# Opening of a spectral filter plus gated MLP kernel: first row tile in two halves on two queues, identity on GpSimd's queue, one dependency less, half a copy on VectorE

## The chip, the cores and the metric

The kernel runs on one core of one Trainium2 chip. The core has TensorE (PE; its weight loads are shown as PEld), VectorE (DVE), ScalarE (ACT), GpSimd (POOL) and SyncE (SP), and 16 DMA engines that SP, ACT and GpSimd can hand transfers to. The metric is the device time of one execution in microseconds (us); several runs are made and their median is given. One execution was also profiled, and that trace is what the prediction reads.

## What is computed

One input x of 2048 tokens by 512 channels (bf16) goes through two branches, whose results are added to it. Branch A layer-normalises x, takes a two-dimensional real FFT, multiplies by a complex filter and transforms back. Branch B is a gated MLP on the same normalised x.

```python
def reference(A_x, A_w_r, A_w_i, B_x, B_w_gate, B_w_up, B_w_down):
    ...
    x = A_x
    xn = _layernorm(x, axis=-1)
    # A: irfft2(rfft2(xn) * (w_r + 1j * w_i))
    # B: (gelu(xn @ w_gate) * (xn @ w_up)) @ w_down
    return x + _A_ref(xn, A_w_r, A_w_i) + _B_ref(xn, B_w_gate, B_w_up, B_w_down)
```

B_x is not used. The gate and up weights are 512 by 1792, the down weight 1792 by 512.

## The kernel before

**Tiling.** x is held as 16 row tiles of 128 partitions by 512 channels: token a*128+q is partition q of tile a. This text calls tile 0 "row one", tile 1 "row two" and so on. For every tile the kernel computes mean and variance on VectorE (`stats`: L520 and L521), the reciprocal root of the variance (`root_act` with ScalarE's square root and VectorE's reciprocal, L525 and L527, for rows one and two; `root_pool` on GpSimd for the others), the normalised tile (`norm`, L537), and its transpose (four 128 by 128 blocks), since TensorE needs channels on partitions. Rows two to four are transposed on TensorE with an identity matrix (`turn`, L550) and copied out of PSUM by VectorE (L555). Rows from five on are transposed by DMA. Row one has its own function, `first_half`, called for h=0 and h=1: 256 channels are normalised (L570), two blocks transposed on TensorE (L567) and copied by ScalarE (L572), so that the first half can go on before the second.

**The matmuls.** The gated MLP is 14 chunks of 128 hidden features by four blocks of four row tiles. `first(3)` starts chunks 0 to 2 on rows one and two as soon as each arrives (L734); everything after that in branch B is `gated` (L715, matmuls with wg and wu, evicted by ScalarE at L720 and L721, multiplied by VectorE at L722) and `down` (L763). Branch A's transforms are matmuls with constant matrices and butterflies on VectorE; TensorE fills the time between them with the MLP. Before its first real work TensorE runs eleven warm-up matmuls on a constant (L476), ten of 512 columns and one of 256.

**The order.** No order is written out. Every operation is declared with an engine, a planned cost, a key, what it reads and writes, and sometimes an explicit predecessor (`after`), a due time, or a planned landing (`land`) for a transfer. `_Sched.run` then lays out all engines in planned time: over all ready operations it takes the one that can start earliest, and among those of the same engine that could start within 0.05 us of it the one with the smallest key (ready time plus the given key, or the due time). This fixes each engine's instruction order. `_Sched.emit` then makes the waits: one semaphore per engine and one per transfer. An operation waits on the semaphores of its predecessors, on its own engine's too, where an older operation's result is read or where `after` names it. An engine runs its queue in order, so an instruction that waits holds all behind it. A changed planned time can change the order anywhere later.

**The transfers of the opening.** On ACT's queue: the identity with one further constant block (`small[:, 0:2]`, 64 KB), then the first 384 columns of wg and of wu. On SP's queue: row one, row two (128 KB each), then, gated behind the fourth warm-up matmul, rows three and four, columns 384 to 768 of wg and wu, rows five to eight, and so on in larger pieces. On GpSimd's queue: no transfer; its first operations are the memsets of `eps` (read by the square root), of `half` (read by `root_pool`) and of the filter's padding (L690).

**The dependency that the change touches.** In the lines

```python
        stats(0, -60.0)
        stats(1, -66.0, None, (sch.ops[-1],))
        root_act(0, 1, -75.0, (sch.ops[-2],))
        root_act(1, 1, -64.0)
```

`sch.ops[-1]` is row one's aggregate (L521), and `sch.ops[-2]` is row two's statistics (L520), so the reciprocal of row one (L527) is declared to come after row two's statistics.

Of the kernel before, what the change touches and what calls it, by code (L numbers as in the profile page):

```python
# [7 lines left out]
ACT = mybir.ActivationFunctionType  # L8
# [7 lines left out]
P = 128  # L16
# [128 lines left out]
class _Sched:  # L145
# [11 lines left out]
    def op(self, eng, cost, fn, reads=(), writes=(), tiles=(), key=0.0, after=(), dma=0, lag=0.0, due=None, land=None):  # L157
        o = _Op()
        o.eng, o.fn, o.cost, o.key, o.dma, o.lag, o.due, o.land = eng, fn, cost, key, dma, lag, due, land
        o.reads, o.writes, o.tiles = reads, writes, [(t, False) for t in tiles]  # L160
        o.extra = [a for a in after if a is not None]
        o.seq = len(self.ops)
        o.end = None
        o.pos = None
        self.ops.append(o)
        return o
# [184 lines left out]
def bass_parallel_sum__spectral_gfnet__glu_gated_geglu__prompt_kernel(  # L351
# [11 lines left out]
    c_small = nc.inline_tensor(small_np, name="c_small")  # L363
# [3 lines left out]
    xb = A_x[0].rearrange("(a q) d -> q a d", q=P)  # L367
# [5 lines left out]
    sch = _Sched()  # L373
    op = sch.op

    with ExitStack() as es:
        def sb(name, shape, dt=BF16, cell=0):
            n = int(np.prod(shape))
            t = es.enter_context(nc.sbuf_tensor(name, [P, n], dt))
            return view(t, name, 0, shape, cell)  # L380
# [13 lines left out]
        x = sb("x_sb", [16, D])  # L394
# [4 lines left out]
        small = sb("smallc", [9, P])  # L399
# [11 lines left out]
        rs = sb("rstd", [16], F32)  # L411
# [49 lines left out]
        def dma(q, dst, src, nbytes, wr=None, rd=None, key=0.0, after=(), cost=0.41, lag=0.0, land=None):  # L461
            after = tuple(after) + tuple(gate if q == "sp" else ())
            return op(q, cost, lambda e: e.dma_start(dst() if callable(dst) else dst.ap, src() if callable(src) else src.ap),
                      reads=rd if rd is not None else (), writes=wr if wr is not None else (), dma=nbytes, key=key, after=after, lag=lag, land=land)
# [16 lines left out]
        def load(q, dst, src, nbytes, **kw):  # L481
            return dma(q, dst, lambda: src, nbytes, wr=(dst,), **kw)

        def wload(q, dst, src, lo, hi, **kw):
            return load(q, dst[:, :, lo:hi], src[:, :, lo:hi], (hi - lo) * 1024, **kw)

        k = iter(np.arange(0.0, 1.0, 0.001))
        def rows(lo, hi, land=None):
            return load("sp", x[:, lo:hi], xb[:, lo:hi, :], (hi - lo) * 131072, key=next(k), land=land)

        load("act", small[:, 0:2].rs([2 * P]), c_small.ap()[:, 0:2 * P], 65536, key=-9)
        for w, v in ((wg, wgv), (wu, wuv)):
            wload("act", w, v, 0, 384, key=0.5, land=5.5 if w is wg else 6.4)
        rows(0, 1)
        rows(1, 2)
        gate.append(warms[3])
        for i in (2, 3):
            rows(i, i + 1, 6.3 + 0.3 * i)
# [14 lines left out]
        def xs(s):  # L513
            return x[:, s]

        def xn(s):
            return RB(8192 + 512 * (s % 8), [4, P])

        def stats(s, key, due=None, after=()):
            op("dve", 0.61, lambda e: e.bn_stats(bst[:, s].ap, xs(s).ap), reads=(xs(s),), writes=(bst[:, s],), key=key, due=due, after=after)  # L520
            op("dve", 0.11, lambda e: e.bn_aggr(bag[:, s].ap, bst[:, s].ap), reads=(bst[:, s],), writes=(bag[:, s],), key=key, due=due)  # L521

        def root_act(s0, n, key, after=()):
            sl = slice(s0, s0 + n)
            op("act", 0.29, lambda e: e.activation(rs.ap[:, sl], bag.ap[:, sl, 1], ACT.Sqrt, bias=eps.ap, scale=1.0),  # L525
               reads=(bag[:, sl], eps), writes=(rs[:, sl],), key=key)
            op("dve", 0.09, lambda e: e.reciprocal(rs.ap[:, sl], rs.ap[:, sl]), reads=(rs[:, sl],), writes=(rs[:, sl],), key=key, after=after)  # L527

        def root_pool(s0, n, key):
            sl = slice(s0, s0 + n)  # L530
# [26 lines left out]
        def first_half(h):  # L557
            cs = slice(2 * h, 2 * h + 2)
            i, r, o = xs(0)[:, 256 * h:256 * h + 256], xn(0)[:, cs].rs([256]), xnT[:, 0, 0, cs].rs([256])
            t = _T("sp")  # L560

            def bank():
                return ps_sp_bf[:, t.slot * 2048:t.slot * 2048 + 256]

            def f(e):
                for j in range(2):
                    ins = e.transpose(bank()[:, j * P:(j + 1) * P], xn(0).ap[:, 2 * h + j], ident.ap)  # L567
                return ins

            op("dve", 0.2, lambda e: e.tensor_scalar(r.ap, i.ap, bag.ap[:, 0, 0:1], rs.ap[:, 0:1], SUB, MUL), reads=(i, bag[:, 0], rs[:, 0:1]), writes=(r,), key=-70.0)  # L570
            op("pe", 2 * 0.107, f, reads=(r, ident), tiles=(t,), key=-70.0, lag=0.1)
            op("act", 0.27, lambda e: e.activation(o.ap, bank(), ACT.Copy), writes=(o,), tiles=(t,), key=-70.0)  # L572

        def turn_dma(s):
            i, o = xn(s), xnT[:, s // 4, s % 4]
# [63 lines left out]

        stats(0, -60.0)  # L640
        stats(1, -66.0, None, (sch.ops[-1],))
        root_act(0, 1, -75.0, (sch.ops[-2],))
        root_act(1, 1, -64.0)
        for h in range(2):
            first_half(h)
# [195 lines left out]
        for v, hh in ((4, (12, 13)), (0, (14, 15)), (2, (8, 9)), (6, (10, 11)), (1, (0, 1)), (7, (4, 6)), (3, (2, 7)), (5, (5, 3))):  # L841
            t = _T("sp")
# [17 lines left out]
        for ri, f in ((0, ADD), (1, SUB)):  # L860
            op("pool", 0.3, lambda e, ri=ri, f=f: e.tensor_tensor(edge.ap[:, ri], ev[0].ap[:, ri], ev[1].ap[:, ri], f),
               reads=(ev[0][:, ri], ev[1][:, ri]), writes=(edge[:, ri],), key=1.0)
# [53 lines left out]
        for i, v in enumerate((0, 4, 1, 7, 2, 6, 3, 5)):  # L916
            t = _T("sp")

            def f_i(e, v=v, t=t):
# [15 lines left out]
               writes=(gv,), tiles=(t,), key=-0.5)  # L935
# [40 lines left out]
        for jq in range(4):  # L976
# [4 lines left out]
            for jp in (2 * jq, 2 * jq + 1):  # L981
                t = _T("sp")
# [57 lines left out]
```

## Time and profile before

| what | value |
|---|---|
| median of 3 runs | 171.54 us (171.25 to 171.77) |
| the profiled execution | 171.33 us, of which 169.5 us is the span from first to last instruction |
| granted TensorE clock, mean | 1.00 |
| DMA, whole kernel | 15.62 MB, mean 92 GB/s |

The opening, by the timeline (start in us from the span's start; the engine's instructions in their order):

| engine | instructions |
|---|---|
| SP, issues | row one 0.72, row two 1.17, row three 2.65, row four 3.02, wg 3.50, wu 3.98 |
| ACT | issues identity 0.72, wg 1.12, wu 1.67; table load 2.29 (1.28 long); root of row one 4.29, of row two 5.29; copies L572 at 6.05 and 6.33 (0.38 each) |
| GpSimd | memsets of eps 0.72, half 0.75, filter 0.79 |
| VectorE | L520 3.35, L521 4.07, L520 4.29, L527 5.02, L521 5.10, L570 5.22 and 5.48 (0.34 each), L527 5.74, L537 5.92, L555 7.03 |
| TensorE | warm-up from 0.76, the last one starts 4.98; L567 5.62 (four), L734 6.49 (two), L550 6.61 (four), L734 from 6.83 |

A row of the profile's group views reads: line, engine, operation, what is written and read (by the kernel's names), shapes, count, then busy time and the mean of one. In a chain of waits each row is start, length and the work that the end of the kernel was waiting for then. "In queue q10" in a DMA view is ACT's queue, q1 is SP's.

### The profile page before, as it was taken

What the parts mean: (1) busy time and instruction counts of PE and PEld (TensorE: products, weight loads), DVE (VectorE), ACT (ScalarE), POOL (GpSimd) and SP (SyncE); (2) the same over time, 40 slices, a digit from 0 to 9 for tenths busy, and PEclk for the clock granted to TensorE, in tenths of its full rate; (3) what the DMA queues carried; (4) which work ended last, traced back from release to release, by engine and by line L of the source; (5) the groups of instructions that cost most, each with busy time, mean ns of one, the idle gap of its engine ahead of it and who ended that gap; (6) DMA issues with size and microseconds to landing.
All of it is one profiled execution on the core that took longest, in us unless ns stands there. A gap on an engine that the chain in (4) does not pass through costs nothing.

```text
span 169.5 us, 2696 instructions
## 1 busy us (share of the span) xinstructions
PE 166.0 (98%) x999; PEld 86.1 (51%) x999; DVE 146.0 (86%) x292; ACT 106.6 (63%) x175; POOL 11.3 (7%) x25
## 2 busy tenths in 40 slices
PE   8899999999999999999999999999999999999994
PEld 3598544445556443444444554644445654444443
DVE  2789999995975999999999999999999969963932
ACT  3688766663979739489663695875738896561000
POOL 2042243500000000010000000000000000000000
PEclk9999999999999999999999999999999999999999
DMA  5999999994025362420000000000000003300322
GB/s 152 333 346 352 283 129 311 216 261 95 0 51 114 84 134 74 116 119 2 0 0 0 0 4 0 0 0 0 4 0 2 0 4 104 128 15 0 124 67 63
DMA packets 22239, 15.62 MB, mean 92 GB/s; under 512 B 9165, under 2 KB 21714, under 8 KB 22226
## 3 DMA queue, kind: packets, MB, share of 16 engines
q1 hardware_dynamic: 21026, 14.60, 34.8%
q10 hardware_dynamic: 1200, 0.85, 1.7%
q8 instruction: 8, 0.13, 0.4%
q14 instruction: 5, 0.04, 0.1%
HBM read 11.38 MB, written 2.10 MB: 80 GB/s over the span
## 4 chain that ended last, share of the span: by engine, by line
PE 95%; DMA 2%; DVE 1%; ACT 0%; issue 0%
PE ps_gu L715 56%; PE ps_dn L763 21%; PE ps_sp L763 7%; PE ps_sp L988 2%; PE ps_sp L632 2%; PE ps_sp L847 2%; DMA x_sb<-in_A_x_dram 2%; PE ps_gu L734 1%; PE ps_sp L928 1%; PE ps_sp L929 1%; DVE bst L520 1%; PE ps_dn L734 1%; PE ps_sp L550 0%; PE ps_sp L851 0%; PE ps_sp L567 0%; ACT xnT L572 0%
## 5 line engine op out<-in xcount | busy, mean ns | idle before, releaser
L715 PE MATMUL ps_gu<-xnT,wg 128*128 128x512 bf16 (+1 forms) x236 | 56.7, 363 | 0.0
L715 PE MATMUL ps_gu<-xnT,wu 128*128 128x512 bf16 (+1 forms) x236 | 56.7, 363 | 0.0
L720 ACT ACTIVATE gg<-ps_gu 128x512 bf16<-128x512 f32 (+1 forms) x59 | 33.7, 572 | 12.2 <-PE ps_gu L715 10.5
L721 ACT ACTIVATE uu<-ps_gu 128x512 bf16<-128x512 f32 (+1 forms) x59 | 33.9, 575 | 10.5 <-PE ps_gu L715 10.2
L763 PE MATMUL ps_dn<-wd,hT 128*128 128x512 bf16 x168 | 38.9, 379 | 0.0
L467 DVE TENSOR_TENSOR specB<-specB 128x512 bf16<-128x512 bf16 (+2 forms) x58 | 33.6, 610 | 1.7 <-ACT specB L993 1.4
L715 PEld LDWEIGHTS ps_gu<-xnT,wu 128*128 128x128 bf16 x236 | 22.9, 98 | 23.0
L715 PEld LDWEIGHTS ps_gu<-xnT,wg 128*128 128x128 bf16 x236 | 22.6, 98 | 22.0 <-ACT uu L721 0.4
L763 PEld LDWEIGHTS ps_dn<-wd,hT 128*128 128x128 bf16 x168 | 16.3, 98 | 19.1
L722 DVE TENSOR_TENSOR hT<-gg,uu 128x512 bf16<-128x512 bf16 (+1 forms) x59 | 23.0, 394 | 1.9 <-ACT uu L721 1.8
L771 ACT ACTIVATE db<-ps_dn 128x512 bf16<-128x512 f32 x12 | 7.2, 597 | 18.4 <-PE ps_dn L763 18.4
L520 DVE BATCH_NORM_STATS2 bst<-x_sb 128x6 f32<-128x512 bf16 x16 | 11.0, 686 | 3.4 <-DMA x_sb<-in_A_x_dram 3.3
L467 DVE TENSOR_TENSOR specC<-specB 128x1024 bf16<-128x1024 bf16 (+2 forms) x18 | 12.4, 713 | 0.2
L763 PE MATMUL ps_sp<-wd,hT 128*128 128x512 bf16 (+2 forms) x70 | 12.3, 336 | 0.0
L467 DVE TENSOR_TENSOR specB<-specA 128x2048 bf16<-128x2048 bf16 x8 | 9.4, 1217 | 2.7 <-ACT specA L637 2.7
L772 DVE TENSOR_TENSOR x_sb<-db,x_sb 128x512 bf16<-128x512 bf16 x12 | 5.0, 418 | 5.3 <-ACT db L771 5.3
L763 PEld LDWEIGHTS ps_sp<-wd,hT 128*128 128x128 bf16 x70 | 6.4, 98 | 6.1 <-DVE x_sb L774 0.2
L467 DVE TENSOR_TENSOR specB<-specB,filt 128x2048 bf16<-128x2048 bf16 x8 | 9.4, 1220 | 0.0
L856 ACT ACTIVATE specA<-ps_sp 128x1024 bf16<-128x1024 f32 x8 | 7.8, 1035 | 1.3 <-PE ps_sp L847 1.3
L637 ACT ACTIVATE specA<-ps_sp 128x1024 bf16<-128x1024 f32 x8 | 7.7, 1023 | 1.2 <-PE ps_sp L632 1.2
L993 ACT ACTIVATE specB<-ps_sp 128x1024 bf16<-128x1024 f32 x8 | 7.8, 1031 | 0.8 <-PE ps_sp L988 0.8
L934 ACT ACTIVATE specC<-ps_sp 128x1024 bf16<-128x1024 f32 x8 | 7.8, 1039 | 0.0
(70 smaller groups left out, 128.8 us busy)
## 6 DMA issues: line engine op xcount, KB each, us to landing
out_dram<-x_sb SPq DMA_DIRECT2D x15, 128.0 KB, 1.8
wd<-in_B_w_down_dram SPq DMA_DIRECT2D x1, 1792.0 KB, 8.4
x_sb<-in_A_x_dram SPq DMA_DIRECT2D x3, 512.0 KB, 8.5
wg<-in_B_w_gate_dram SPq DMA_DIRECT2D x2, 512.0 KB, 8.6
wu<-in_B_w_up_dram SPq DMA_DIRECT2D x2, 512.0 KB, 9.2
toki<-c_ti SPq DMA_DIRECT2D x1, 768.0 KB, 4.4
tokf<-c_tf SPq DMA_DIRECT2D x1, 576.0 KB, 4.8
x_sb<-in_A_x_dram SPq DMA_DIRECT2D x4, 128.0 KB, 3.5
```

What stands on the lines that cost most here:

```text
L467: return op("dve", c_tt(n), lambda e: e.tensor_tensor(o.ap, a.ap, b.ap, f), reads=(a, b), writes=(o,), key=key, **kw)
L520: op("dve", 0.61, lambda e: e.bn_stats(bst[:, s].ap, xs(s).ap), reads=(xs(s),), writes=(bst[:, s],), key=key, due=due, after=after)
L637: op("act", c_act(1024), lambda e, yv=yv, t=t: e.activation(yv.ap, spair(t).rearrange("p (s r i) -> p s i r", s=4, r=4), ACT.Copy), writes ...
L715: ins = e.matmul(gub(t, n), w.ap[:, dc, fc * P:(fc + 1) * P], xnT.ap[:, b, sl, dc, :], start=(dc == 0), stop=(dc == 3))
L720: op("act", c_act(n), lambda e: e.activation(gg.ap[:, gs.slot, 0:n], gub(g, n), ACT.Gelu_apprx_tanh), tiles=(g, gs), key=0.0)
L721: op("act", c_act(n), lambda e: e.activation(uu.ap[:, us.slot, 0:n], gub(u, n), ACT.Copy), tiles=(u, us), key=0.0)
L722: op("dve", c_tt(n), lambda e: e.tensor_tensor(hT.ap[:, h.slot, lo:lo + n], gg.ap[:, gs.slot, 0:n], uu.ap[:, us.slot, 0:n], MUL), tiles=(g ...
L763: ins = e.matmul(bank(), hT.ap[:, hs[(b, fc)].slot, sl * P:(sl + 1) * P], wd.ap[:, fc, lo:lo + n], start=(fc == 0), stop=(fc == NFC - 1))
L771: op("act", c_act(n), lambda e: e.activation(db.ap[:, d.slot, 0:n], bank(), ACT.Copy), tiles=(t, d), key=0.0)
L856: op("act", c_act(1024), lambda e, xv=xv, t=t: e.activation(xv.ap, spair(t), ACT.Copy), writes=(xv,), tiles=(t,), key=-0.5)
L934: op("act", c_act(1024), lambda e, gv=gv, t=t: e.activation(gv.ap, spair(t).rearrange("p (k x i) -> p k x i", k=4, x=4), ACT.Copy), writes ...
L993: op("act", c_act(1024), lambda e, rv=rv, t=t: e.activation(rv.ap, spair(t), ACT.Copy), writes=(rv,), tiles=(t,), key=-0.5)
```

## The change

- Row one is loaded in two transfers of 64 partitions (64 KB each): partitions 0 to 63 on SP's queue, 64 to 127 on ACT's queue, each the first of its queue. ACT's identity load moves to GpSimd's queue, with the smallest key there, so ahead of the memsets.
- The plan gets landings: identity 4.0, the halves of row one 3.1, row two 3.7 us.
- `root_act` loses its `after` argument, so row one's reciprocal no longer names row two's statistics as a predecessor.
- In `first_half`, the copy of half h=0 out of PSUM is a VectorE `tensor_copy`; the copy of h=1 stays on ScalarE.

```diff
-        load("act", small[:, 0:2].rs([2 * P]), c_small.ap()[:, 0:2 * P], 65536, key=-9)
+        load("pool", small[:, 0:2].rs([2 * P]), c_small.ap()[:, 0:2 * P], 65536, key=-9, land=4.0)
+        for q, h in (("sp", 0), ("act", 1)):
+            l = slice(64 * h, 64 * h + 64)
+            load(q, x[l, 0], xb[l, 0, :], 65536, key=-9, land=3.1)
         for w, v in ((wg, wgv), (wu, wuv)):
             wload("act", w, v, 0, 384, key=0.5, land=5.5 if w is wg else 6.4)
-        rows(0, 1)
-        rows(1, 2)
+        rows(1, 2, 3.7)
...
-        def root_act(s0, n, key, after=()):
+        def root_act(s0, n, key):
...
-            op("dve", 0.09, lambda e: e.reciprocal(...), reads=(rs[:, sl],), writes=(rs[:, sl],), key=key, after=after)
+            op("dve", 0.09, lambda e: e.reciprocal(...), reads=(rs[:, sl],), writes=(rs[:, sl],), key=key)
...
-            op("act", 0.27, lambda e: e.activation(o.ap, bank(), ACT.Copy), writes=(o,), tiles=(t,), key=-70.0)
+            if h:
+                op("act", 0.27, lambda e: e.activation(o.ap, bank(), ACT.Copy), writes=(o,), tiles=(t,), key=-70.0)
+            else:
+                op("dve", 0.2, lambda e: e.tensor_copy(o.ap, bank()), writes=(o,), tiles=(t,), key=-70.0)
...
-        root_act(0, 1, -75.0, (sch.ops[-2],))
+        root_act(0, 1, -75.0)
```

More of the change, by code (lines that the diff above doesn't have):

```diff
@@ L526, in root_act @@
                reads=(bag[:, sl], eps), writes=(rs[:, sl],), key=key)
-            op("dve", 0.09, lambda e: e.reciprocal(rs.ap[:, sl], rs.ap[:, sl]), reads=(rs[:, sl],), writes=(rs[:, sl],), key=key, after=after)
+            op("dve", 0.09, lambda e: e.reciprocal(rs.ap[:, sl], rs.ap[:, sl]), reads=(rs[:, sl],), writes=(rs[:, sl],), key=key)
         def root_pool(s0, n, key):
```

## The prediction

> **What bounds the kernel now.** I read four views, in this order. The page's busy shares and its chain of waits come first, to see which engine carries the time:
>
> ```profile
> PE 166.0 (98%) x999; PEld 86.1 (51%) x999; DVE 146.0 (86%) x292; ACT 106.6 (63%) x175; POOL 11.3 (7%) x25
> ...
> PE 95%; DMA 2%; DVE 1%; ACT 0%; issue 0%
> ```
>
> Then the waits of TensorE alone, from 6.4 us to the end. It has one row:
>
> ```profile
> PE ps_gu L734 <- ACT xnT L572: 0.2, 1, 0.2
> ```
>
> From its first real matmul at 6.49 us TensorE never waits again: it runs to 167.3, and one last VectorE add and one store follow. So 171.33 (the profiled execution) is 6.49 of opening, 160.8 of unbroken matmuls, 2.2 of tail inside the 169.5 span, and 1.8 around the span. Two things can move the time: the moment the unbroken stream begins, and a hole torn into it. The change touches only loads and operations of the opening, so the third view is the chain in order of time (start, length, what):
>
> ```profile
> 0.72 2.60 DMA x_sb<-in_A_x_dram
> 3.32 0.02 issue
> 3.35 0.70 DVE bst L520
> 4.05 0.02 issue
> 4.07 0.19 DVE bag L521
> 4.27 0.02 issue
> 4.29 0.70 DVE bst L520
> 4.99 0.02 issue
> 5.02 0.16 DVE rstd L527
> 5.18 0.08 DVE bag L521
> 5.26 0.31 DVE specB L570
> 5.57 0.05 issue
> 5.62 0.41 PE ps_sp L567 x2
> 6.02 0.02 issue
> 6.05 0.39 ACT xnT L572
> 6.44 0.05 issue
> 6.49 0.29 PE ps_gu L734 x2
> 6.77 0.22 PE ps_sp L550 x4
> ```
>
> The reader is to see two links that are not row one's own work: row two's statistics (4.29), and row two's transposes L550, which stand on TensorE between the first two L734 matmuls and the other L734. The last view, the DMA issues in narrow windows, gives landings one by one: row one issued 0.72, landed 2.6 later; the identity (ACT's queue) 2.4; row two, issued 1.17, 2.8, so at 4.0; the second piece of wu, issued on SP at 3.98, 5.6:
>
> ```profile
> wu<-in_B_w_up_dram SPq DMA_DIRECT2D x1, 384.0 KB, 5.6
> ```
>
> So that piece lands at 9.60, and the timeline has TensorE's weight load for it at 9.73. This is the tightest later arrival; the next, rows 5 to 8, has over 1 us in hand.
>
> **The change part by part.** *Row one in halves.* Each of 16 DMA engines carries eight 1 KB pieces of row one, 46 ns each in the packet records: 0.37 us in one queue or two. What goes is the identity from in front: eight 512 B pieces of 27 ns, 0.22 us per engine, mixed between. Bounds: 0 (both halves must land, the later counts) to 0.27. I take 0.20, near the 0.22: landing 3.12, statistics at 3.15. Issue costs nothing: ACT still issues three transfers (0.36 and 0.53 and 0.53 before its table load at 2.29, done 3.57, needed at 4.1), SP still two before its gate. [...]
>
> *Row two's load* keeps its place on SP, second. Its statistics want it at 4.09 now (3.15 plus the 0.72 and 0.22 between the old starts 3.35, 4.07, 4.29), and it landed at 4.0 with 64 KB more ahead of it: cost 0, cover 0.05 to 0.1.
>
> *The reciprocal.* Only the explicit dependency goes. Working the planner's greedy rule by hand (order only, no times): row two's statistics may start when row one's aggregate ends, while the root is still on ACT, so VectorE's order stays statistics two, reciprocal, aggregate two, halves. What goes is the wait on statistics two's completion. An operation that waits for an older result starts about 0.08 before its predecessor ends (the two L570, 0.34 long, start 0.26 apart); so the reciprocal starts at 4.09+0.61=4.70 rather than 4.82, and the first half at 4.90 (old spacing from the reciprocal 0.20). Gain so far 0.20+0.12=0.32: 5.22 to 4.90. The transposes follow 0.40 later as before, at 5.30. The warm-up matmuls cover down to there: the last, half-size one starts at 4.98 and they start 0.43 apart, so the array is free near 5.19. That floor bounds this part to 0.4.
>
> *Copy of half one on VectorE.* The trace has no such copy. Below: 0.28 (hT, 128x256); above: 0.42 (L555, 128x512 from the same PSUM). I take 0.30, nearer the smaller, equal in elements. Against ACT's 0.38 it gains 0.08. Transposes 5.30, plus the old 0.43: copy 5.73 to 6.03, first L734 at 6.08 rather than 6.49, a gain of 0.41. But what is queued behind the copy on VectorE is row two's normalisation L537. By the same hand working it comes after the copy, because the reciprocal of row two is ready just after the transposes of half one. It sat at 5.92; it now starts at 5.73+0.22=5.95, ends 6.36, and row two's transposes can load at 6.41 (they loaded at 6.55). They stay ahead of the rest of L734 on TensorE. So TensorE waits some 0.2 after its two early matmuls and the unbroken stream gains only 6.55-6.41=0.14. ACT's copy of half two (5.96 to 6.34) is hidden behind that.
>
> *Identity on GpSimd's queue.* It is issued ahead of eps, mhalf and the filter memset, which move behind it. eps is wanted at 4.1, mhalf at 8.8, so this costs nothing unless the issue takes over 3 us. The transposes want the identity at 5.30; it could come at 5.65 before the stream starts later than now (identity +0.05, transposes 0.43, copy 0.30, 0.05, two matmuls 0.13, against 6.61). No row has a GpSimd transfer. Below: as on ACT, 0.72+2.4=3.1. Above: GpSimd needs 0.58 to 0.72 for a one-column power where a VectorE reciprocal takes 0.16, four times; four times ACT's 0.36 issue, then the 4.2 of rows three and four, which waited behind ACT's weights: 0.72+1.4+4.2=6.3. I take 4.5 (that issue, then 2.4): cost 0. [...]
>
> *Later arrival.* The DMA engines are full from 2.2 us on (windows 2.2 to 12: share 0.87 to 1.11) and the bytes ahead of the second wu piece are the same, so it still lands at about 9.60. After the semaphore's 0.03 its weight load can start from 9.63 to 9.66 rather than 9.73. Of the 0.14, this lets through 0.07. From there the stream is as before.
>
> **Sum.** 0.14 gained at the start of the stream, 0.07 given back at the weights: 171.33-0.07=171.26 for the profiled execution, which stands 0.21 under the median; 171.54-0.07 = **171.47**. Its own range is 171.3 to 171.6. A difference of 0.3% (0.51 us) is about what a measurement of this kernel can tell from none.
>
> **Rivals.**
>
> *Halves bring nothing:* the later half lands at 3.32. Everything shifts 0.20, row two's transposes load at 6.61, 0.06 late: 171.6. For it: the same 0.37 us of engine work; against: the identity's pieces in front.
>
> *The gain passes:* wu lands a little earlier and the early start counts. 0.14 up to 0.37 (transposes from 5.62 to 5.25, if row two's normalisation hides too): 171.17 to 171.4, centre 171.3; the spread of single runs (171.25 to 171.77) could carry it past 0.3%. Against: 9.60 and 9.73.
>
> *Identity late, slower:* place, TensorE's wait before L567; it decides from a landing after 5.65, then us for us. [...] In the window 3.9 to 4.4 only ACT's queue moved packets, though row three had been issued on SP at 2.65. If GpSimd's transfer gets its turn only after ACT's two weight pieces (landed 5.2 and 6.5), it lands at 6.3: +0.65, 172.2. Against: 1.1 us of margin at my value.
>
> *Row two late, slower:* the smaller first transfers let ACT's wg (issued 1.12) pass row two (issued 1.17). VectorE's queue holds the reciprocal behind its statistics; it costs from a start after 4.23. One wg piece ahead is 1.2 us of engines (landings of wg and wu 1.3 apart): landing 5.2 at worst, +1.0, 172.5; half of it 172.0. Against: it went first before.
>
> *The order moves:* the whole plan is computed anew and its opening is earlier by more than the chip's, while the due times of later statistics stay. A hole in TensorE's stream of 0.3 to 1 us would give 171.9 to 172.5; for it, VectorE is full from 12 to 40 us (27.75 of 28); against it, TensorE has filler work to 155.
>
> **Chances.** Forecast 0.31, halves nothing 0.08, gain passes 0.18 (0.08 of it beyond 0.3%), identity late 0.20 (0.14), row two late 0.12 (0.08), order 0.11 (0.08 slower, 0.02 faster). Faster 0.10, slower 0.30, within 0.60. Range 171.1 to 172.3: it leaves out most of the fast tail and the worst of the two late arrivals.
>
> **What would show it.** Right: statistics at 3.15, first L570 at 4.9, first L734 near 6.1, a wait of 0.2 on TensorE before L550, L550's load at 6.4, and a short wait near 9.6 before L715 with wu. Wrong: L567 waiting for a DMA (identity), the second L520 idle for x_sb (row two), L537 ahead of the copy (my planner reading), or any TensorE wait after 12 us (order).

## The result, and the profile after

The changed kernel takes 174.33 us (median of 6 runs, 174.24 to 174.69) against 171.40 (6 runs, 171.25 to 171.77): a ratio of 1.0173 (1.0159 to 1.0187). The forecast was 171.47, the range 171.1 to 172.3; the time lies above both. The profiled execution took 174.69 us with a span of 172.8, so 3.3 us more span than before. The page of the changed kernel, busy time and the shares of its chain of waits:

```profile
PE 167.8 (97%) x999; PEld 87.7 (51%) x999; DVE 145.8 (84%) x293; ACT 107.3 (62%) x174; POOL 12.8 (7%) x26
...
PE 94%; DMA 3%; DVE 1%; SPq 0%; issue 0%; DVEq 0%
```

TensorE still carries the kernel, with as many matmuls as before, yet it is busy 1.8 us longer: the same instructions took more time. ScalarE has left the chain (its copy has gone to VectorE), and SP's queue has come into it. The waits of TensorE after its warm-up, for the changed kernel (engine, what it waited for, then sum, times and longest in us):

```profile
PE ps_sp L569 <- DVE specB L572: 1.9, 1, 1.9
```

One wait is all there is; before there were two of 0.2 each, before L567 and L734 (L569 and L739 after the change). What it waited for is told by the chain in order of time of the changed kernel (start, length, what):

```profile
0.73 0.59 SPq L463
...
1.37 4.60 DMA x_sb<-in_A_x_dram
...
6.06 0.69 DVE bst L522
6.76 0.06 DVE rstd L529
...
6.97 0.24 DVE specB L572
...
7.26 0.30 PE ps_sp L569 x2
...
7.58 0.30 DVE xnT L577
...
7.93 0.28 PE ps_gu L739 x2
...
8.25 0.40 PE ps_sp L552 x4
```

Read it from the load: the transfer issued at 1.37 is row two. It landed at 5.97, where it had landed at 4.01. Row two's statistics (the L522 at 6.06) stand on VectorE ahead of row one's reciprocal (L529), so row one, whose halves had landed at 3.17 and 2.87, waited too. TensorE, done with its warm-up at 5.4, had nothing until 7.26. The transposes of row two (L552), from which on the stream is unbroken, began at 8.25 instead of 6.61: **1.64 us** of the 3.3.

The rest is in the granted clock. Windows of the changed kernel (from:to, length, then busy time with instructions of PE, PEld, DVE, ACT, POOL, and at the end PEclk, DMA share, GB/s):

```profile
5.44:8.85 3.41, 1.42 (x17) 0.94 (x18) 2.24 (x9) 1.29 (x3) 0.00 (x0) 1.00 1.10 338
8.85:12.27 3.42, 3.42 (x36) 3.42 (x34) 2.43 (x6) 1.53 (x4) 1.61 (x4) 0.50 1.10 344
```

From 8.85 on, 1.6 us after the gap had ended, TensorE ran for 3.41 us at a granted clock of 0.50; its 128-column matmuls stand 0.107 apart there (8 in 0.85 us) instead of 0.056 (16 in 0.89 us in the kernel before, at a granted clock of 1.00). Half of 3.41 is **1.7 us**. 1.64 + 1.7 = 3.34, against 3.3 measured. All six runs show a mean clock of 0.99, which is what one such stretch makes of 172 us (1 - 0.5 x 3.41 / 172).

Why did row two land late? The issues in the engines' timelines (start, length of the issuing instructions; a row with x2 spans row one's or its half's issue and row two's). The kernel before:

```profile
0.72 0.39 SPq L463 DMA_DIRECT2D x_sb<-in_A_x_dram  x1
...
0.72 0.87 SPq L463 DMA_DIRECT2D x_sb<-in_A_x_dram  x2
...
0.72 0.36 ACTq L463 DMA_DIRECT2D smallc<-c_small  x1
1.12 0.53 ACTq L463 DMA_DIRECT2D wg<-in_B_w_gate_dram  x1
```

The changed kernel:

```profile
0.73 0.59 SPq L463 DMA_DIRECT2D x_sb<-in_A_x_dram  x1
...
0.73 1.45 SPq L463 DMA_DIRECT2D x_sb<-in_A_x_dram  x2
...
0.74 0.55 ACTq L463 DMA_DIRECT2D x_sb<-in_A_x_dram  x1
1.32 0.59 ACTq L463 DMA_DIRECT2D wg<-in_B_w_gate_dram  x1
```

An issue of a 64-partition half takes 0.59 on SP and 0.55 on ACT; before, SP needed 0.39 for the whole row and ACT 0.36 for the identity. Behind them row two's issue runs from 1.37 to 2.18 (before: 1.18 to 1.59) and wg's from 1.32 to 1.92 (before: 1.12 to 1.65). By starts wg was ahead in both kernels; by ends the order has turned round. What the queues then moved, in the DMA view of the window 2.8 to 4.0 us (packets, MB, share of the 16 engines; q10 is ACT's queue, q1 SP's, q0 GpSimd's). The kernel before:

```profile
q10 hardware_dynamic: 316, 0.24, 66.0%
q1 hardware_dynamic: 141, 0.12, 32.9%
```

The changed kernel:

```profile
q10 hardware_dynamic: 151, 0.12, 44.6%
q0 software_dynamic: 22, 0.03, 23.3%
```

Row two stood first in SP's queue then, and in these 1.2 us not one packet of that queue moved. Nor did wg make use of it: the three queues together left a third of the engines' time unused (0.68, before 0.99). Some 0.21 MB were not moved in this window that were before (0.36 against 0.15), 0.6 us at the 345 GB/s that follow. That is the lateness of all later arrivals: wg 5.77 (before 5.15), the first wu piece 7.15 (6.48), the second 10.31 (9.60). In the changed kernel the late stream hides them.

### The profile page after: what moved, and what is told of

It reads as the page before. It is cut to its first block, busy times and chain, and to the rows that moved or that the text cites. A ratio compares the mean times of both kernels' runs of the same rounds, so it can differ in the third digit from the quotient of the medians.

```text
span 172.8 us, 2698 instructions
## 1 busy us (share of the span) xinstructions
PE 167.8 (97%) x999; PEld 87.7 (51%) x999; DVE 145.8 (84%) x293; ACT 107.3 (62%) x174; POOL 12.8 (7%) x26
## 4 chain that ended last, share of the span: by engine, by line
PE 94%; DMA 3%; DVE 1%; SPq 0%; issue 0%; DVEq 0%
PE ps_gu L720 55%; PE ps_dn L768 21%; PE ps_sp L768 7%; DMA x_sb<-in_A_x_dram 3%; PE ps_sp L993 2%; PE ps_sp L637 2%; PE ps_gu L739 2%; PE ps_sp L852 2%; PE ps_sp L933 1%; PE ps_sp L934 1%; PE ps_dn L739 1%; PE ps_sp L552 0%; DVE bst L522 0%; SPq L463 0%; PE ps_sp L856 0%
## 5 line engine op out<-in xcount | busy, mean ns | idle before, releaser
L720 PE MATMUL ps_gu<-xnT,wu 128*128 128x512 bf16 (+1 forms) x236 | 56.7, 363 | 0.0
L720 PE MATMUL ps_gu<-xnT,wg 128*128 128x512 bf16 (+1 forms) x236 | 56.7, 363 | 0.0
L720 PEld LDWEIGHTS ps_gu<-xnT,wu 128*128 128x128 bf16 x236 | 22.8, 98 | 23.0 <-ACT specA L861 0.4
L720 PEld LDWEIGHTS ps_gu<-xnT,wg 128*128 128x128 bf16 x236 | 22.8, 98 | 22.5
L522 DVE BATCH_NORM_STATS2 bst<-x_sb 128x6 f32<-128x512 bf16 x16 | 10.9, 682 | 5.2 <-DMA x_sb<-in_A_x_dram 5.2
```

What stands on the lines that cost most here:

```text
L720: ins = e.matmul(gub(t, n), w.ap[:, dc, fc * P:(fc + 1) * P], xnT.ap[:, b, sl, dc, :], start=(dc == 0), stop=(dc == 3))
```

## The experiments

Times are medians; each ratio is against runs of the kernel before on the same chip. "Row two" experiments first, then the clock, then the parts. Every kernel computes the whole result.

**Row two ahead of wg.** Theory A of these runs is that the issues' order makes row two late; the rival B is the GpSimd transfer.

```diff
+        load("act", x[:, 1:2], xb[:, 1:2, :], 131072, key=-8, land=3.7)
         for w, v in ((wg, wgv), (wu, wuv)):
...
-        rows(1, 2, 3.7)
```

> The changed kernel with row two issued on ACT's queue ahead of wg, all else kept, GpSimd's transfer too. Theory A (wg passed row two among the transfers of SP and ACT, which are served in order of issue): row two lands by 4.1, second L522 starts by 4.15, stream starts near 6.5, no half clock, time 171.2 to 171.8. Rival B (GpSimd's transfer holds the DMA engines up): row two still lands after 4.7 and time stays above 172.5.

Measured: 172.26, 1.0046 (1.0028 to 1.0064). Row two's line in its DMA issues (KB, us from issue to landing):

```profile
x_sb<-in_A_x_dram ACTq DMA_DIRECT2D x1, 128.0 KB, 2.8
```

It landed at 4.16 and row two's transposes came at 6.55. This trace has no record of the clock; its 128-column matmuls stand 0.056 apart from 6.6 on, as in the kernel before at its clock of 1.00, so this is full speed. So the order alone takes the loss from 1.73% to 0.46%, with the partition halves and the GpSimd transfer both left in. The time is still above the expectation, and the timeline of TensorE in this kernel says why (start, length, count, and in brackets the idle time before and what ended it):

```profile
8.11 0.62 PE L739 MATMUL ps_gu<-xnT,wu 128*128 128x128 bf16 x8 [0.60 <-DMA wu<-in_B_w_up_dram]
```

With row two in time the later weights are the bound: wu landed at 8.06, behind all that had been moved ahead of it.

**No transfer on GpSimd.** The identity goes on SP's queue behind row two; halves as in the change.

```diff
-        load("pool", small[:, 0:2].rs([2 * P]), c_small.ap()[:, 0:2 * P], 65536, key=-9, land=4.0)
...
         rows(1, 2, 3.7)
+        load("sp", small[:, 0:2].rs([2 * P]), c_small.ap()[:, 0:2 * P], 65536, key=next(k), land=4.0)
```

> The changed kernel without a transfer on GpSimd: the identity is issued on SP behind row two, all engine orders of the compute engines the same. Theory A: wg still passes row two, which lands after 5.0, time 173 to 174.5. Rival B: row two lands near 3.8 as nothing holds it up, time under 172.

Measured: 174.98, 1.0202 (1.0161 to 1.0242), a little over the 173 to 174.5 that A gave. VectorE's timeline in this kernel:

```profile
5.80 0.69 DVE L522 BATCH_NORM_STATS2 bst<-x_sb 128x6 f32<-128x512 bf16 x1 [1.59 <-DMA x_sb<-in_A_x_dram]
```

Row two is still late (5.71) with GpSimd out of it, and a stretch of half clock follows (9.17 to 12.58). B falls.

**Halves by columns.** The same two transfers of 64 KB on the same two queues, but all 128 partitions by 256 channels each.

```diff
-            l = slice(64 * h, 64 * h + 64)
-            load(q, x[l, 0], xb[l, 0, :], 65536, key=-9, land=3.1)
+            l = slice(256 * h, 256 * h + 256)
+            load(q, x[:, 0, l], xb[:, 0, l], 65536, key=-9, land=3.1)
```

> The changed kernel with row one halved by columns (128 partitions by 256 columns on each queue) instead of by partitions; every engine's order is the same. Theory A, made narrower by the runs so far (it is the 64-partition shape whose issue takes 0.59 and 0.55 us instead of 0.39 and 0.36, so that wg's issue ends before row two's): issues back to 0.36 to 0.42, row two issued near 1.15, landed by 4.0, second L522 near 4.1, stream start near 6.45, clock 1.00, time 171.1 to 171.6. Rival E (any second half on ACT pushes row two behind wg): row two lands after 5, time over 173.

Measured: 171.75, 1.0017 (1.0001 to 1.0033). The issues take 0.39 and 0.41, row two's ends at 1.60 and wg's at 1.62, and row two landed at 3.69. The shape of the halves is thus what turned the order, and nearly the whole loss goes with it. VectorE's timeline in this kernel is the opening that was predicted:

```profile
3.14 0.69 DVE L522 BATCH_NORM_STATS2 bst<-x_sb 128x6 f32<-128x512 bf16 x1 [3.14 <-DMA x_sb<-in_A_x_dram]
...
4.09 0.69 DVE L522 BATCH_NORM_STATS2 bst<-x_sb 128x6 f32<-128x512 bf16 x1
4.70 0.15 DVE L529 RECIPROCAL rstd<-rstd 128x1 f32<-128x1 f32 x1
...
4.91 0.57 DVE L572 TENSOR_SCALAR specB<-x_sb,bag,rstd 128x256 bf16<-128x256 bf16 x2
...
5.80 0.29 DVE L577 COPY xnT<-ps_sp 128x256 bf16<-128x256 bf16 x1 [0.24 <-PE ps_sp L569]
6.01 0.40 DVE L539 TENSOR_SCALAR specB<-x_sb,bag,rstd 128x512 bf16<-128x512 bf16 x1
```

The stream began at 6.46, 0.15 earlier than before, and is not faster in the end: the second wu piece landed at 9.81 (before 9.60) and TensorE stood 0.16 for it.

**The identity first on ACT again, partition halves kept.**

```diff
-        load("pool", small[:, 0:2].rs([2 * P]), c_small.ap()[:, 0:2 * P], 65536, key=-9, land=4.0)
+        load("act", small[:, 0:2].rs([2 * P]), c_small.ap()[:, 0:2 * P], 65536, key=-10, land=4.0)
```

> The changed kernel, halves by partitions kept, but the identity first on ACT's queue again, so that wg is issued after it and after the half, near 1.7, behind row two. Theory A (order of issue decides): row two lands by 4.3 although the halves have the 64-partition shape, no half clock, time 171.6 to 172.6, since wg and wu come some 0.5 us later. Rival I (the 64-partition shape itself delays the next transfers, whoever is first): row two after 5, time over 173.

Measured: 172.93, 1.0091 (1.0058 to 1.0124), over the expectation. Now ACT issues the identity, its half (0.64 long) and only at 1.79 wg; row two's issue (from 1.35) ends first again. Its DMA issues, row two and ACT's half:

```profile
x_sb<-in_A_x_dram SPq DMA_DIRECT2D x1, 128.0 KB, 2.8
...
x_sb<-in_A_x_dram ACTq DMA_DIRECT2D x1, 64.0 KB, 2.8
```

Row two landed at 4.14, as the order of the issues' ends says, with two 64-partition issues in the kernel. But ACT's half, second in its queue, landed at 3.88, so row one's statistics began at 3.98 and row two's transposes at 7.22. The expectation's "no half clock" was wrong. TensorE's timeline in this kernel:

```profile
7.62 0.85 PE L739 MATMUL ps_gu<-xnT,wg 128*128 128x128 bf16 x6
...
8.69 1.06 PE L739 MATMUL ps_gu<-xnT,wu 128*128 128x128 bf16 x8
```

These matmuls start 0.107 apart, as in the changed kernel at a granted clock of 0.50, so at half speed, until about 9.8. This is not the stretch of the changed kernel: the speed was not lost but came late. The warm-up's 512-column matmuls stand 0.43 apart here as in every trace (0.22 is full speed: 14 of L763 in 3.02 us in the kernel before, at a granted clock of 1.00), and a spacing of 0.056 does not come before 9.8. From row two's transposes to the end this trace takes 164.1 us, 1.2 more than the kernel before (169.5 - 6.61 = 162.9), about half of the 2.5 us that they and the matmuls behind them spent at half speed. The view shows a clock of 1.00 throughout because this trace, too, has no record of it, so the spacing is the evidence. Why full speed came so late, and in how many of the other three runs, is not known.

**Longer warm-up**, by four and by eight matmuls of 512 columns in the last warm-up operation. This adds work and changes nothing else.

```diff
+            def f(e):
+                for _ in range(4 if n == 256 else 0):
+                    e.matmul(ps_dn[:, 0:512], ones[:, 0:P], ones[:, 0:512], start=True, stop=True)
+                return e.matmul(ps_dn[:, 0:n], ones[:, 0:P], ones[:, 0:n], start=True, stop=True)
```

Four:

> The changed kernel with four more 512-column warm-up matmuls inside the last warm-up operation, so TensorE is kept busy to about 6.9 us; nothing else differs, and row two is as late as in the changed kernel. Theory C (half of the loss is the clock, which was granted at 0.5 from 8.9 to 12.3 us after TensorE idled from 5.4 to 7.3): granted clock 1.00 all through, about 1.6 to 1.7 us gained, 172.6. Rival D (the loss is all waiting): 174.3 as the changed kernel.

Eight:

> As the run with four more warm-up matmuls, but with eight more, so that TensorE is busy until row one's transposes at about 7.3 us. Theory C: granted clock 1.00 after the warm-up in every run, a span near 171.3 and a median of 172.4 to 173.2, with less spread than with four. Rival D (the loss is all waiting): 174.3.

Measured: four, 174.07, 1.0154 (1.0110 to 1.0199), the runs from 173.26 to 175.18 and not all at full clock; eight, 173.56, 1.0114 (1.0099 to 1.0129), all with a mean clock of 1.00. With four the median is nearer to the 174.3 of rival D than to the 172.6 of theory C and decides nothing; the run that was traced (173.26) had no half-clock stretch. The four ended at 6.5 already, because the clock rose at 6.0 (from 4.99 to 6.36 they stand 0.34 apart in the mean, against 0.43). The stretch of the gap and nearly the same window as above, in the kernel with eight:

```profile
5.20:7.20 2.00, 2.00 (x9) 0.74 (x7) 0.54 (x1) 0.00 (x0) 0.00 (x0) 1.00 1.10 351
...
8.85:12.25 3.40, 3.40 (x56) 3.34 (x57) 2.76 (x7) 2.73 (x7) 1.29 (x4) 1.00 1.10 342
```

The gap is filled, the clock stays at 1.00, and 56 matmuls start in the window that held 36. Row two came still later in this kernel (6.56), so its transposes began at 8.85, 0.60 after those of the changed kernel; its span is 1.03 shorter all the same. The clock was therefore worth 0.60 + 1.03 = 1.63, beside the 1.7 worked out above. The same count in the other traces agrees: from row two's transposes to the end it is 162.9 us in the kernel before, with four, with eight and with the two edits alone (below), and 164.5 to 164.6 in the changed kernel and in the one without a GpSimd transfer, the two traces with the half-clock stretch. The time is above the expected 172.4 to 173.2 by what row two was later.

**Row one's chain ahead of row two's statistics.** A planned landing of 6.0 for row two puts its statistics behind row one's reciprocal and halves in VectorE's order.

```diff
-        rows(1, 2, 3.7)
+        rows(1, 2, 6.0)
```

> The changed kernel with row two's planned landing at 6.0 in place of 3.7, so that the planner puts row one's reciprocal, halves and copies ahead of row two's statistics on VectorE; transfers as in the changed kernel. Theory F (the late row two costs so much because row one's chain stands behind its statistics on VectorE): first L739 near 6, row one's matmuls done while row two is awaited, row two's transposes near 8, about 1.57 us of row-one matmuls already done by then, time 172.0 to 172.8 if the clock stays at 1.00. Rival G (row two itself is the bound, whatever the order): 174 or more.

Measured: 174.09, 1.0145 (1.0130 to 1.0160), as rival G had it; theory F fell. Row one's transposes did come at 5.20, and the profile shows full clock. The waits of TensorE in this kernel show where the gain went:

```profile
PE ps_gu L739 <- DMA wg<-in_B_w_gate_dram: 0.9, 1, 0.9
PE ps_gu L720 <- DVE xnT L557: 0.7, 1, 0.7
PE ps_gu L739 <- DVE xnT L557: 0.5, 1, 0.5
PE ps_gu L739 <- DMA wu<-in_B_w_up_dram: 0.3, 1, 0.3
```

wg landed at 6.62 in this run, so the transposed row one had no weights, and then row two was missing. With this order of issues the loads, not VectorE's order, are late.

**The prediction's gains alone:** the kernel before with the dependency dropped and the copy on VectorE, all loads as before.

```diff
-            op("act", 0.27, lambda e: e.activation(o.ap, bank(), ACT.Copy), writes=(o,), tiles=(t,), key=-70.0)
+            if h:
+                op("act", 0.27, lambda e: e.activation(o.ap, bank(), ACT.Copy), writes=(o,), tiles=(t,), key=-70.0)
+            else:
+                op("dve", 0.2, lambda e: e.tensor_copy(o.ap, bank()), writes=(o,), tiles=(t,), key=-70.0)
...
-        root_act(0, 1, -75.0, (sch.ops[-2],))
+        root_act(0, 1, -75.0)
```

> Loads as before the change; only the reciprocal's dependency is gone and half one is copied on VectorE. The prediction's sum without the halves: first half 0.12 us earlier, first L737 (the old L734) near 6.3, row two's transposes within 0.1 us of the old 6.55, time 171.3 to 171.6. If the two edits were a cost by themselves (a TensorE hole after 12 us from the new order): 172 or more.

Measured: 171.49, 0.9998 (0.9975 to 1.0020). Its chain in order of time:

```profile
5.83 0.30 DVE xnT L575
...
6.18 0.28 PE ps_gu L737 x2
...
6.50 0.40 PE ps_sp L550 x4
```

Both edits do what was said of them (first gated matmul 6.18 instead of 6.49, row two's transposes 6.50 instead of 6.61), and the 0.1 us that the stream begins earlier is less than these runs can tell.

**The identity on GpSimd alone:** the kernel before with only that move; so that ACT's later issues keep their places, ACT issues a load of the same 64 KB to a buffer that nothing reads.

```diff
-        load("act", small[:, 0:2].rs([2 * P]), c_small.ap()[:, 0:2 * P], 65536, key=-9)
+        load("pool", small[:, 0:2].rs([2 * P]), c_small.ap()[:, 0:2 * P], 65536, key=-9, land=4.0)
+        spare = sb("spare", [2 * P])
+        load("act", spare, c_small.ap()[:, 0:2 * P], 65536, key=-9)
```

> The kernel before, with only the identity moved to GpSimd's queue; ACT first loads the same 64 KB into a spare buffer that nothing reads, so that SP's and ACT's issues keep their order (64 KB more are moved). Theory A (the move by itself does not delay row two): row two lands by 4.1, identity between 3.9 and 5.5, time 171.4 to 172.0. Rival B again (GpSimd's transfer is what hurts): row two after 4.7, time over 172.5.

Measured: 172.04, 1.0028 (1.0001 to 1.0055), with 64 KB more to move. Row two landed at 3.68, so this part does not delay it. But in the profiled execution the identity itself was late. A line of its DMA issues:

```profile
smallc<-c_small POOLq DMA_DIRECT2D x1, 64.0 KB, 5.1
```

It landed at 6.27, and row one's transposes, whose halves were ready, began at 6.41; row two's at 7.28 instead of 6.61. In the other traces with this transfer it landed between 3.85 and 5.40.

**Halves by columns, identity on ACT behind its half:** the changes of "halves by columns" and

```diff
-        load("pool", small[:, 0:2].rs([2 * P]), c_small.ap()[:, 0:2 * P], 65536, key=-9, land=4.0)
...
+        load("act", small[:, 0:2].rs([2 * P]), c_small.ap()[:, 0:2 * P], 65536, key=-8, land=4.0)
```

> A candidate: halves by columns, the identity on ACT's queue behind its half, nothing on GpSimd, the other edits of the changed kernel kept. Row one lands near 3.0, row two near 3.8, identity by 4.0, stream start 6.4, second wu piece near 9.7 (a wait of up to 0.15): 171.2 to 171.7. If wg, issued near 1.6, then lands after 6.1, the first L739 waits for it: 171.8 or more.

Measured: 172.15, 1.0040 (1.0023 to 1.0056); the expectation was missed. It has the earliest stream of all (6.29; row one landed at 3.00, row two at 3.69, the identity at 3.85). The waits of TensorE's weight loads in this kernel:

```profile
PEld ps_gu L720 <- ACT uu L754: 0.7, 1, 0.7
...
PEld ps_gu L739 <- DMA wu<-in_B_w_up_dram: 0.3, 1, 0.3
```

wg could only be issued at 1.65, wu landed at 7.33 and the second wu piece at 10.29. The first row names ACT, but ACT's operation there was long done; the weights that L720 loads landed at 10.29, 0.13 before it went on. The stream is 0.3 early at its head and stands 0.29 and 0.59 at the two pieces of wu. No kernel of these is faster than the one before; the one with the two edits alone equals it.

## Why the prediction was wrong

**The step that failed** is "Row two's load keeps its place on SP, second ... cost 0", and under it "Issue costs nothing: ACT still issues three transfers ..., SP still two before its gate". The transfers were counted and their issues were not: a half cost 0.59 and 0.55 instead of 0.39 and 0.36, the next issue on SP 0.81 instead of 0.42. The order in which wg and row two came to the DMA engines hung on some 0.05 us (ends near 1.59 and 1.65). In place of cost 0 the step measured 1.96 us at the landing and 1.64 at the stream. Three runs show the cause: with row two put ahead (172.26), with halves of another shape (171.75), with ACT's queue delayed (row two at 4.14) it lands in time again; without the GpSimd transfer (174.98) it does not.

**The rival "row two late"** had the right place (the statistics idle for x_sb, the reciprocal queued behind them) and the right cause, wg passing row two. Its price was wrong in two terms. "Landing 5.2 at worst" took wg for one block of 1.2 us of full engines; the engines were only 0.68 busy in the window 2.8 to 4.0, and row two landed 0.8 later than that worst case. And a gap on TensorE was priced as its length alone, +1.0 at worst: it measured 1.9, which made the stream 1.64 later, and the clock term of 1.7, more than that, was in no sum. With chance 0.12 and a ceiling of 172.5, the true time lay outside everything that was put down.

**The other terms held**, by the kernel with halves by columns, where row two is in time: statistics 3.14 (said: 3.15), second statistics 4.09 (4.09), reciprocal 4.70 (4.70), first half 4.91 (4.90), copy 5.80 long 0.29 (5.73, 0.30), normalisation of row two behind the copy at 6.01 (5.95), row two's transposes 6.46 (6.41). In the changed kernel VectorE's order was the predicted one too. That the earlier stream is given back at the second wu piece was right in kind, by the 0.16 that TensorE stood there with halves by columns; with the two edits alone, where that piece landed at 9.58, the trace shows no such wait. The landing "still at about 9.60" was not right: 9.81, 10.29 and, in the changed kernel, 10.31 where the head of the queues was rearranged, so the later weights take back all of it.

**The identity** landed where it was forecast in the changed kernel (4.44, said 4.5), in part by luck: its issue began at 1.17, not 0.72, and took 0.75, not 1.4. And the bound of 6.3 was no mere bound: 6.27 was measured in another. That rival, hidden here by row two, cost 0.28% in the kernel with that move alone.

**The split by itself** was not run. The kernel nearest to it is the one with partition halves and the identity first on ACT again: it differs from the one with the two edits alone by the halves and their planned landings, and has 1.0091 against 0.9998. There the second half stood behind the identity (landed at 3.88), and a part of the loss is the late full speed.

## What to carry to other kernels

When two queues feed the same DMA engines (here ACT's took 66.0% and SP's 32.9% of the 16 from 2.8 to 4.0 us in the kernel before), write down when each issue ends, not only how many there are: row two landed at 4.01 where its issue ended before wg's (1.59 and 1.65), at 5.97 where it ended after it (2.18 and 1.92). A load that the first results hang on should win that order by more than a few hundredths, or stand ahead in the same queue. If a row tile like this one must be split, split it by columns (issues of 0.39 and 0.41 us here) rather than partitions (0.55 to 0.64), and check its issue time first. Price a gap on TensorE early in a kernel with the half-clock stretch that may follow it (here 3.41 us at a clock of 0.50 after a gap of 1.9, so 1.7 us; none in the trace with a gap of 1.2), and a gain at the head with the next weights to arrive (0.15 gained with halves by columns, 0.16 stood at the second wu piece).

## What the runs showed of the hardware that was not expected

- **Issue time goes with the shape.** 64 KB as 64 partitions by 512 channels took 0.55 to 0.64 us to issue, as 128 partitions by 256 channels 0.39 to 0.41. Why is not shown.
- **Order between two queues.** In every trace with the two on different queues, that of row two and wg went first whose issue *ended* first, be it by under 0.03 us (1.60 and 1.62 with halves by columns). Where that was row two, or where it stood ahead in wg's own queue, row two landed at 3.68 to 4.16 (seven traces); where it was wg, at 5.71 to 6.56 (five traces), and what makes that spread is open. That the end decides is read from these cases, and was not tried by itself. Service strictly in order of issue, as theory A of the run with row two ahead of wg puts it, is not what the windows show throughout. In the kernel before SP's queue moved no packet from 3.9 to 5.0, though row three's issue began at 2.65, and then 91 from 5.0 to 6.0 beside ACT's 379, with wu not yet landed (6.48). In the changed kernel SP's moved 100 from 4.0 to 5.0 beside ACT's 372. Between 2.8 and 4.0 there SP's moved none, though row two had been issued by 2.18 and the engines were 0.68 busy; whether the engines had its work by then is not shown. What kept them from more is open, and it was not GpSimd's transfer alone: without it they were 0.73 busy in the same window.
- **The clock.** Half clock came in a stretch of 3.41 us in two traces (8.85 to 12.27, 9.17 to 12.58). In the changed kernel the 3.41 us before the stretch were not idle throughout: they held 1.42 us of busy TensorE, behind a gap of 1.9 us. What sets the stretch off and what ends it is not shown. With the identity alone on GpSimd a gap of 1.2 us brought none in the trace. The start differs from trace to trace as well: the warm-up begins at the same point (0.76 in the kernel before, 0.77 in the changed one), and full speed is on record from 5.44 us in the changed kernel and from 6.07 in the kernel before; by the spacing of the matmuls it came at 6.0 with four more in the warm-up, and at about 9.8 with the identity first on ACT.
- **GpSimd's transfer** of 64 KB landed 2.7 to 5.1 us after its issue, from the same place in GpSimd's program; what sets it was not settled.
